# A third weight piece moved behind the evictions, and two value scalings moved between GpSimd and VectorE

## The chip, the core and the metric

The kernel runs on one core of a Trainium2 chip. The metric is device time in microseconds (us) of one execution, median over several runs. The engines are named as the profile names them: PE is TensorE's matrix unit and PEld its weight loads, DVE is VectorE, ACT is ScalarE, POOL is GpSimd, SP is SyncE, which issues most of the DMAs.

## What is computed

Two parts follow each other. The first is a linear attention ("retention") with a decay per head, over 4 batches, 8 heads, 768 positions and head width 64:

```python
for t in range(S):
    state = gamma[None, :, None, None] * state + np.einsum('bhd,bhe->bhde', k[:, :, t], v[:, :, t])
    y[:, :, t] = scale * np.einsum('bhd,bhde->bhe', q[:, :, t], state)
```

Its 3072 rows of 512 numbers go into a layer of 8 experts, where each row goes to one expert only:

```python
logits = x @ w_gate
expert_idx = np.argmax(logits, axis=1)
# probs = softmax(logits); gate_w = probs of the chosen expert
for e in range(E):
    xe = x[expert_idx == e]
    out[expert_idx == e] = gate_w[expert_idx == e, None] * (np.maximum(xe @ w1[e], 0.0) @ w2[e])
```

## The kernel before

**Chunks and periods.** The attention is cut into 24 chunks of 128 positions (6 for a batch). The loop over `n` (line 615) makes 12 periods, 0 to 11, of two chunks each, `a = 2n` and `b = 2n + 1`. The recurrence over positions is turned into matmuls: `scores` (line 278) multiplies keys and queries into the PSUM banks `sp`, and DVE masks them into `Sb` (line 287); `update` (line 293) adds a chunk to the state `U`, which ACT copies to `ub`; `carry` (line 313) multiplies the queries with the state into the PSUM tile `Y`, and `output` (line 330) adds the chunk's own part. `evict` (line 340) takes `Y` out of PSUM on DVE, into `xT`. The decay is carried by scaling: `scale` (line 265) multiplies a chunk's values by powers of gamma, and its result `vs` is read by `update` and `output`. There is one buffer for `Y`: the first matmul of `carry` for a period cannot start before both evictions of the period before have read it.

**Order.** The order is written by hand: every engine runs its instructions in the order in which the code names them, so an instruction that waits holds back all that follow it on its engine. POOL's queue holds most of the scalings, one for a chunk, and the scatter DMAs that send finished rows (line 853), with short dummy instructions between sends (`pause`, line 201, tile `idle`).

**What fills the gaps.** Beside the attention, the weights of the first expert are prepared: `split` (line 142) has ACT cast a piece of a loaded weight to `whi`, and an engine of the caller's choice subtracts it into `wlo` (line 148). `SPLITS` names the pieces of each period; period 7 has three, all subtracted on DVE: the first at line 640, the other two at line 648, ahead of `output` in the code and so ahead of the evictions on DVE.

**The early rows.** In period 9 (`soon`), after the send of chunk 17, SP fetches the rows already known to belong to the first expert (`fetch_early`, line 526, tile `xg`). In period 11 DVE transposes them (line 868), ACT casts them to `xh` (line 875), and PE begins that expert with them (line 908) before the attention has ended. The seven other experts follow from line 1131 on, and take most of the run.

**Which engine scales which chunk.** Chunk 0 is scaled in halves, heads 0 to 3 on POOL, heads 4 to 7 on DVE (line 290, between two maskings). All others are scaled on POOL by `scale`: chunk 1 near the start (line 606), chunks 21 and 22 together at the end of period 9 (lines 708 and 710).

Of the kernel before, what the change touches and what calls it, by code (L numbers as in the profile page):

```python
# [10 lines left out]
F32 = mybir.dt.float32  # L11
# [7 lines left out]
B, H, S, D = 4, 8, 768, 64  # L19
E, DM, F = 8, 512, 1024  # L20
N = B * S
P = 128
# [38 lines left out]
SPLITS = {n: tuple(next(_ORDER) for _ in range(c)) for n, c in _PIECES.items()}  # L61
# [48 lines left out]
def retention_moe(ctx, tc, front, qkv, w1, w2, first_rows, second_rows, out):  # L110
    nc = tc.nc
# [30 lines left out]
    def split(pos, part, i, engine, n=2):  # L142
        if i == 0:
            wparts[pos, part] = [wp.tile([P, 4, 512], F32R, name=n, tag="w", bufs=11) for n in ("whi", "wlo")]
        raw, (hi, lo) = raws[pos, part], wparts[pos, part]
        h = slice(n * i, n * i + n)
        nc.scalar.copy(out=hi[:, h], in_=raw[:, h])  # L147
        engine.tensor_tensor(out=lo[:, h], in0=raw[:, h], in1=hi[:, h].bitcast(F32), op=ALU.subtract)  # L148
# [74 lines left out]
    with ExitStack() as actx:  # L223
        apool = lambda name, bufs, **kw: actx.enter_context(tc.tile_pool(name=name, bufs=bufs, **kw))
        ld = apool("ld", AHEAD)
        wk = apool("wk", 2)
# [22 lines left out]
        def turned(g, i):  # L249
            return qs[g][:, i].rearrange("a (p t) -> a p t", p=NP)  # L250
# [6 lines left out]
        scaled = {}  # L257

        def scale_heads(g, engine, h):
            v, powers = (qs[g][:, 2], cv[:, g % CPB, :]) if g else (head[:, 0:DM], head[:, DM:DM + H])  # L260
            engine.tensor_tensor(
                out=scaled[g][:, h], in0=v.rearrange("a (h d) -> a h d", d=D)[:, h],
                in1=powers[:, h].unsqueeze(2).broadcast_to([P, h.stop - h.start, D]), op=ALU.mult)

        def scale(g):
            c = g % CPB
            vs = scaled[g] = wk.tile([P, H, D], F32, name="vs", bufs=3)
            scale_heads(g, nc.gpsimd, slice(0, H if g else H // 2))
            vss[g] = vs.rearrange("a (n t) d -> a n (t d)", t=2)
            if g == 1:  # L270
                double(2)
            if g == c and g > 0:
                grow(c)
# [4 lines left out]
        def scores(g):  # L278
            Sb = wk.tile([P, 2, NP, C], F32, name="Sb")
            q, kt = turned(g, 0), turned(g, 1)  # L280
            sps = [bank(2 * (g % 2) + r, "sp") for r in range(2)]
            for p in range(NP):
                for r in range(2):
                    nc.tensor.matmul(out=sps[r][:, p, :], lhsT=kt[half[r], p, :], rhs=q[half[r], p, :],  # L284
                                     start=True, stop=True)
            for r in range(2):
                nc.vector.tensor_tensor(out=Sb[:, r], in0=sps[r],  # L287
                                        in1=causal.unsqueeze(1).broadcast_to([P, NP, C]), op=ALU.mult)
                if g == 0 and r == 0:
                    scale_heads(0, nc.vector, slice(H // 2, H))  # L290
            Sbs[g] = Sb

        def update(g):
# [16 lines left out]
        def begin(n):  # L310
            Ys[n] = ps_1.tile([P, 2, DM], F32, name="Y", tag="Y")
# [28 lines left out]
        def evict(g):  # L340
            Y, c = Ys[g // 2], g % CPB
            if g % 2 == 0:
                xTs[g // 2] = wk.tile([P, NP, TW], F32, name="xT")
            xT = xTs[g // 2][:, :, (g % 2) * C:(g % 2 + 1) * C]
            nc.vector.tensor_tensor(out=xT.rearrange("a (r m) t -> a r m t", m=2), op=ALU.mult,
                                    in0=Y[:, :, 2 * (g % 2) * C:2 * (g % 2 + 1) * C].rearrange("a r (m t) -> a r m t", m=2),
                                    in1=G[:, c].rearrange("a (r m) t -> a r m t", m=2))
# [264 lines left out]
        soon = FULL // 2  # L612
        stages = {}

        for n in range(last + 1):
            a, b = 2 * n, 2 * n + 1
            s = gating(chosen[n]) if n in chosen else None
            if s:
                stages[chosen[n]] = s
            begin(n)  # L620
            if n == soon:
                logits(n - 1)
            else:
                if n == 0:
                    output(a)
                carry(n)
            if n > 0:
                if n == last:
                    turn_early()
                if n != soon:  # L630
                    logits(n - 1)
                if n == last:
                    for j, w, _ in first["pieces"]:
                        cut_high(nc, first["x"][0], first["xt"], j, w)
                if n in AMID:
                    send_behind(state["LT"][:, 0:1], AMID[n])
                rows(a - 2, "s0")
                rows(a - 1, "s1")
                finish_logits(n - 1)
            for i in SPLITS[n][:1 if n == 7 else None] if n in (6, 7) else ():  # L640
                split(0, *i, nc.gpsimd if n == 6 else nc.vector, 1)
            if s and n < last:
                s["choose"]()
            if n == soon:
                carry(n)
            if b % CPB < CPB - 1:
                update(b)
            for i in SPLITS[n][1:] if n == 7 else ():
                split(0, *i, nc.vector, 1)
            if s and n < last:  # L650
                s["soft"]()
            if n > 0:
                output(a)
            if n == soon:
                s["rank"]()
            output(b)
            if n == soon:
                for name in ("slots", "weights", "label", "counts"):
                    s[name]()
                nc.vector.tensor_copy(out=filled, in_=full)  # L660
                nc.vector.tensor_scalar(out=s0, in0=full, scalar1=base, scalar2=float(EARLY), op0=ALU.subtract,
                                        op1=ALU.min)
                nc.vector.tensor_tensor(out=start, in0=s0, in1=base, op=ALU.add)
                send_apart(range(FULL - 2, FULL))
                fill_late()
                fetch_early()
            elif s and n < last:
                s["rank"]()
                s["slots"]()
                if n == GROUPS[0][1] // 2:  # L670
                    s["totals"]()
            for g in (a, b):
                evict(g)
            if n == last:
                cut_early()
                s["choose"]()
            elif s:
                for name in ("weights", "label")[2 * (n == soon):] + ("advance",):
                    s[name]()
            if n == soon - 1:  # L680
                scale(b + 2)
                scale(a + 4)
            if n in BEHIND:
                send_behind(xTs[n][:, 0, C:C + 1], BEHIND[n],
                            pause if n == soon - 1 else lambda: [scale(g) for g in ((b + 2, a + 4) if n == soon - 2 else (b + 2,))])
            if n == 1:
                nc.vector.tensor_scalar(out=run, in0=k_("ebase"), scalar1=1.0 / P, scalar2=None, op0=ALU.mult)
            if n < last:
                if n > 0:
                    update(a + 2)  # L690
                if n in AFTER:
                    pause()
                    send_behind(ubs[(a + 2) % 3][:, 0, 0:1], AFTER[n])
                scores(a + 2)
                if n == 0:
                    update(a + 2)
                scores(b + 2)
            if n == GROUPS[0][1] // 2:
                s["pick"]()
                expert_at[0] = nc.sync.value_load(first_at[0:1, 0:1], min_val=0, max_val=E - 1)  # L700
                fetch(0, 0)
                fill_rows()
                fetch(0, 2)
            if n == 0:
                nc.scalar.copy(out=wgs[:, :, 0:E], in_=k_("gates").rearrange("p (k e) -> p k e", k=NP))
            if n < last:
                if n not in BEHIND:
                    scale(b + 2)
                if n < last - 1 and n not in (soon - 2, soon - 1):
                    scale(a + 4)  # L710
            for i in SPLITS.get(n, ()) if n > 7 else ():
                split(0, *i, nc.gpsimd, 1)
            for g in (a, b):
                if FIRST <= g < NCH - AHEAD - len(MID):
                    load(g + AHEAD + len(MID))
                if g in fetches:
                    fetch(0, fetches[g])
                for i in LATER.get(g, ()):
                    load(i)
# [650 lines left out]
```

## Time and profile before

| | us |
|---|---|
| median of 3 runs | 381.54 (381.48 to 381.74) |
| the profiled execution, its own time | 379.4 |
| its span, from the first instruction to the last | 377.6 |
| PE busy in the span | 371.0 (98%) |
| POOL busy | 260.3 (69%) |
| DVE busy | 251.7 (67%) |
| ACT busy | 140.5 (37%) |

The mean granted TensorE clock was 0.997. The page says where time is spent in total. The rows further down are from the list of instructions in order of time: a row gives start and duration in us, engine, line, operation, `out<-in` and shape, the count of instructions merged into the row, and in square brackets how long the engine was idle before it and what ended that. A row's end is its start plus its duration. The end of a matmul row is modelled; back to back, a row starts a little before the modelled end of the one before.

### The profile page before, as it was taken

How to read it: one execution, taken by the hardware profiler on the slowest of the kernel's cores; microseconds unless marked ns; L12 is line 12 of the kernel's file. 1: busy time of each engine (PE TensorE's matmuls, PEld its weight loads, DVE VectorE, ACT ScalarE, POOL GpSimd, SP SyncE). 2: the span in 40 equal slices, each digit the busy share in tenths (PEclk: the TensorE clock that was granted, in tenths of full speed). 3: DMA queues.
4: the chain of work that ended last, by engine and by line, in shares of the span. 5: the costliest groups of instructions: out<-in, count | busy, mean ns of one | idle time of the engine just before them, and what ended most of it. 6: DMA issues, size and time to landing. Idle time of an engine off the chain costs nothing. (4 is left out here: it accounts for less than half of the span.)

```text
span 377.6 us, 8710 instructions
## 1 busy us (share of the span) xinstructions
PE 371.0 (98%) x3279; PEld 349.3 (93%) x3279; DVE 251.7 (67%) x496; ACT 140.5 (37%) x252; POOL 260.3 (69%) x278
## 2 busy tenths in 40 slices
PE   8999999999999999999999999999999999999994
PEld 5888888788899899999999999999999999999984
DVE  3467858877778866768784777576676668667211
ACT  2222344244541645534630543154235316424200
POOL 3751669988760299008996999499569929987873
PEclk9999999999999999999999999999999999999998
DMA  7999999986249597869646754846457557520102
GB/s 305 417 414 420 416 402 423 417 353 172 92 159 201 197 240 252 262 217 277 223 145 115 231 162 141 194 166 210 133 149 224 176 91 251 184 101 24 38 20 80
DMA packets 42031, 82.06 MB, mean 217 GB/s; under 512 B 4268, under 2 KB 17584, under 8 KB 39537
## 3 DMA queue, kind: packets, MB, share of 16 engines
q1 hardware_dynamic: 36656, 67.67, 54.4%
q0 software_dynamic: 5312, 13.49, 10.0%
q8 instruction: 47, 0.77, 0.9%
q14 instruction: 16, 0.12, 0.1%
HBM read 65.80 MB, written 15.85 MB: 216 GB/s over the span
## 5 line engine op out<-in xcount | busy, mean ns | idle before, releaser
L853 POOL DMA_INDIRECT out<-Z,sidx x88 | 100.9, 1147 | 63.9 <-DVE Z L1061 49.2
L148 DVE TENSOR_TENSOR wlo<-raw,whi 128x1024 fp32r<-128x1024 f32 (+1 forms) x63 | 74.0, 1178 | 16.5 <-ACT whi L147 16.2
L203 POOL TENSOR_TENSOR idle<-cs 1x256 bf16<-1x256 f32 x102 | 79.6, 780 | 2.8
L147 ACT CAST whi<-raw 128x1024 fp32r<-128x1024 f32 (+1 forms) x72 | 67.7, 951 | 5.8 <-DMA raw<-w 5.8
L1218 PE MATMUL py<-hh,whi 128*128 128x392 f32 (+4 forms) x192 | 65.7, 342 | 0.0
L1218 PE MATMUL py<-hl,whi 128*128 128x392 f32 (+4 forms) x192 | 65.7, 342 | 0.0
L1218 PE MATMUL py<-hh,wlo 128*128 128x392 f32 (+4 forms) x192 | 65.7, 342 | 0.0
L1193 ACT ACTIVATE hh<-ph 128x452 fp32r<-128x452 f32 (+6 forms) x56 | 28.4, 507 | 77.6 <-PE ph L1186 77.1
L1186 PE MATMUL ph<-xh,wlo 128*128 128x392 f32 (+5 forms) x224 | 49.0, 340 | 0.0
L1186 PE MATMUL ph<-xl,whi 128*128 128x392 f32 (+5 forms) x224 | 48.9, 340 | 0.0
L1186 PE MATMUL ph<-xh,whi 128*128 128x392 f32 (+5 forms) x224 | 48.9, 340 | 0.0
L1194 DVE SCALAR_TENSOR_TENSOR hl<-ph,hh 128x452 fp32r<-128x452 f32 (+6 forms) x56 | 32.1, 574 | 20.3 <-ACT hh L1193 19.5
L1186 PEld LDWEIGHTS ph<-xh,whi 128*128 128x128 f32 x224 | 40.2, 188 | 0.4
L1186 PEld LDWEIGHTS ph<-xl,whi 128*128 128x128 f32 x224 | 40.3, 188 | 0.2
L1186 PEld LDWEIGHTS ph<-xh,wlo 128*128 128x128 f32 x224 | 40.2, 188 | 0.1
L1218 PEld LDWEIGHTS py<-hl,whi 128*128 128x128 f32 x192 | 36.1, 188 | 0.2
L1218 PEld LDWEIGHTS py<-hh,wlo 128*128 128x128 f32 x192 | 36.1, 188 | 0.2
L1218 PEld LDWEIGHTS py<-hh,whi 128*128 128x128 f32 x192 | 36.0, 188 | 0.2
L287 DVE TENSOR_TENSOR Sb<-sp,cs 128x512 f32<-128x512 f32 x48 | 29.9, 681 | 5.9 <-PE sp L284 5.9
L875 ACT CAST xh<-buf 128x512 fp32r<-128x512 f32 (+6 forms) x24 | 13.3, 558 | 51.5 <-DVE buf L868 51.5
L853 POOL DMA_INDIRECT x_sorted<-xrow,KEY x24 | 24.9, 1037 | 6.9 <-issue 4.1
L1056 DVE STREAM_TRANSPOSE Z<-py 128x416 f32<-128x416 f32 (+3 forms) x24 | 15.0, 625 | 18.9 <-PE py L1218 18.5
(200 smaller groups left out, 555.6 us busy)
## 6 DMA issues: line engine op xcount, KB each, us to landing
raw<-w SPq DMA_DIRECT2D x32, 1024.0 KB, 6.1
qkv_w<-qkv SPq DMA_DIRECT2D x12, 1024.0 KB, 17.7
qkv_t<-qkv SPq DMA_DIRECT2D x7, 1024.0 KB, 15.1
qkv_t<-front SPq DMA_DIRECT2D x7, 512.0 KB, 7.5
buf<-x_sorted SPq DMA_DIRECT2D x12, 211.2 KB, 5.2
x_sorted<-cs SPq DMA_DIRECT2D x7, 260.0 KB, 5.5
buf<-x_sorted SPq DMA_DIRECT2D x8, 195.0 KB, 3.9
out<-Z,sidx POOLq DMA_INDIRECT x88, 3.6
```

The lines of the kernel that those rows point to most:

```text
L147: nc.scalar.copy(out=hi[:, h], in_=raw[:, h])
L148: engine.tensor_tensor(out=lo[:, h], in0=raw[:, h], in1=hi[:, h].bitcast(F32), op=ALU.subtract)
L203: nc.gpsimd.tensor_tensor(out=idle[0:1], in0=cs[0:1, 0:PAUSE], in1=cs[0:1, 0:PAUSE], op=ALU.mult)
L287: nc.vector.tensor_tensor(out=Sb[:, r], in0=sps[r], in1=causal.unsqueeze(1).broadcast_to([P, NP, C]), op=ALU.mult)
L853: sc = tc.nc.gpsimd.indirect_dma_start(out=dst, out_offset=bass.IndirectOffsetOnAxis(ap=index, axis=0), in_=rows, in_offset=None, bounds_c ...
L875: nc.scalar.copy(out=xh[:, :, c0:c0 + w], in_=xt[:, :, t0:t0 + w])
L1056: nc.vector.transpose(out=Zs[e][:, 0:nb, k, :], in_=py[:, 0:32 * nb].rearrange("p (j c) -> p j c", c=32))
L1186: nc.tensor.matmul(out=ph[:, :w], lhsT=wparts[e, f // 4][a][:, kd, fo:fo + P], rhs=x[:, kd, :w], start=(n == 0), stop=(n == 3 * KD - 1))
L1193: nc.scalar.activation(out=hh[:, :cap], in_=ph[:, :cap], func=AF.Relu)
L1194: nc.vector.scalar_tensor_tensor(out=hl[:, :cap], in0=ph[:, :cap], scalar=0.0, in1=hh[:, :cap].bitcast(F32), op0=ALU.max, op1=ALU.subtract)
L1218: nc.tensor.matmul(out=py[:, :c], lhsT=a[:, f % 4, k * P:(k + 1) * P], rhs=x[:, :c], **se)
```

## The change

Three places change. The third weight piece of period 7 is no longer subtracted ahead of that period's evictions but behind them, and the two matching ACT casts keep their order. Chunk 21 is scaled on DVE, at the same place in the code, which on DVE is behind the four maskings of period 9. Chunk 1 is scaled in halves as chunk 0 was: heads 0 to 3 on POOL, heads 4 to 7 on DVE between the two maskings of chunk 1. Nothing is computed differently.

```diff
         def scale_heads(g, engine, h):
+            if g not in scaled:
+                scaled[g] = wk.tile([P, H, D], F32, name="vs", bufs=3)
...
-        def scale(g):
+        def scale(g, engine=nc.gpsimd):
             c = g % CPB
-            vs = scaled[g] = wk.tile([P, H, D], F32, name="vs", bufs=3)
-            scale_heads(g, nc.gpsimd, slice(0, H if g else H // 2))
+            scale_heads(g, engine, slice(0, H // 2 if g < 2 else H))
+            vs = scaled[g]
...
-                if g == 0 and r == 0:
-                    scale_heads(0, nc.vector, slice(H // 2, H))
+                if g < 2 and r == 0:
+                    scale_heads(g, nc.vector, slice(H // 2, H))
...
-            for i in SPLITS[n][1:] if n == 7 else ():
+            for i in SPLITS[n][1:2] if n == 7 else ():
                 split(0, *i, nc.vector, 1)
...
             for g in (a, b):
                 evict(g)
+            for i in SPLITS[n][2:] if n == 7 else ():
+                split(0, *i, nc.vector, 1)
...
-                    scale(b + 2)
+                    scale(b + 2, nc.vector if n == soon else nc.gpsimd)
```

DVE at the end of period 7, before: masking of chunks 14 and 15, the reduction of the logits, the three pieces, the two evictions, and the masking of chunks 16 and 17 (the names `Sb`, `wlo` and `xT` are those of the section on the kernel; `lg` holds logits).

```order
L287 TENSOR_TENSOR Sb<-sp,cs 128x512 x4
L408 TENSOR_REDUCE lg_1120<-lp 128x16
L148 TENSOR_TENSOR wlo<-raw,whi 128x512 x3
L345 TENSOR_TENSOR xT<-Y,buf 128x4x128 x2
L287 TENSOR_TENSOR Sb<-sp,cs 128x512 x4
```

DVE at the same place, after (all lines behind the edits are numbered two to four higher):

```order
L289 TENSOR_TENSOR Sb<-sp,cs 128x512 x4
L410 TENSOR_REDUCE lg_1121<-lp 128x16
L148 TENSOR_TENSOR wlo<-raw,whi 128x512 x2
L347 TENSOR_TENSOR xT<-Y,buf 128x4x128 x2
L148 TENSOR_TENSOR wlo<-raw,whi 128x512
L289 TENSOR_TENSOR Sb<-sp,cs 128x512 x4
```

One piece stands between the evictions and the maskings now, where it stood ahead of the evictions.

POOL from the last sends of period 9 to the weight pieces, before: the send of chunk 17 is the last DMA, the two scalings behind it are chunks 21 and 22.

```order
L853 DMA x_sorted<-xrow,KEY 25600x520 x2
L203 TENSOR_TENSOR idle<-cs 1x256
L853 DMA x_sorted<-xrow,KEY 25600x520
L261 TENSOR_TENSOR vs<-qkv_t,cs 128x512 x2
L148 TENSOR_TENSOR wlo<-raw,whi 128x512 x2
```

DVE at the end of period 9, after: evictions of chunks 18 and 19, a sum of counts, the masking of chunks 20 and 21, the scaling, and period 10's logits.

```order
L347 TENSOR_TENSOR xT<-Y,buf 128x4x128 x2
L470 TENSOR_REDUCE tot_1478<-EA 128x8
L289 TENSOR_TENSOR Sb<-sp,cs 128x512 x4
L263 TENSOR_TENSOR vs<-qkv_t,cs 128x512
L410 TENSOR_REDUCE lp<-lp 128x16
```

One `vs` has left POOL, where chunk 22's now follows the send at once, and stands on DVE behind the maskings.

## Rows read from the trace of the kernel before

**Rows 1.** Waits of PE: line, waited for whom, us, times, longest.

```profile
PE U L301 <- POOL vs L261: 0.3, 1, 0.3
PE Y L323 <- DVE xT L345: 0.3, 1, 0.3
```

**Rows 2.** In order of time, end of period 7 (columns as told above).

```profile
64.86 2.06 PE L284 MATMUL sp<-qkv_t 64*128 64x128 f32 x32
...
65.81 1.27 DVE L345 TENSOR_TENSOR xT<-Y,buf 128x512 f32<-128x512 f32 x2
66.22 0.60 POOL L203 TENSOR_TENSOR idle<-cs 1x256 bf16<-1x256 f32 x1
66.98 1.02 POOL L853 DMA_INDIRECT x_sorted<-xrow,KEY  x1 [0.16 <-issue]
67.01 2.47 DVE L287 TENSOR_TENSOR Sb<-sp,cs 128x512 f32<-128x512 f32 x4
67.23 1.10 PE L323 MATMUL Y<-qkv_t,ub 64*64 64x128 f32 x32 [0.32 <-DVE xT L345]
...
68.84 1.10 PE L356 MATMUL tr<-cs,xT 128*128 128x128 f32 x8
```

**Rows 3.** The same join of PE one period earlier, without a wait.

```profile
58.19 1.06 PE L284 MATMUL sp<-qkv_t 64*128 64x128 f32 x16
...
59.18 0.67 PE L323 MATMUL Y<-qkv_w,ub 64*64 64x128 f32 x16
```

**Rows 4.** In order of time, end of period 9 and start of period 10.

```profile
81.74 2.47 DVE L287 TENSOR_TENSOR Sb<-sp,cs 128x512 f32<-128x512 f32 x4
...
83.58 1.01 POOL L853 DMA_INDIRECT x_sorted<-xrow,KEY  x1 [0.16 <-issue]
...
84.62 2.05 POOL L261 TENSOR_TENSOR vs<-qkv_t,cs 128x512 f32<-128x512 f32 x2
...
85.02 0.38 PE L402 MATMUL lp<-cs,LT 128*128 128x128 f32 x2
...
85.73 0.69 PE L301 MATMUL U<-vs,qkv_t 128*64 128x64 f32 x16 [0.33 <-POOL vs L261]
```

**Rows 5.** The early rows' way to PE, in order of time.

```profile
87.10 2.96 SPq L157 DMA_DIRECT2D xg<-x_sorted  x4
...
92.96 1.30 DVE L868 STREAM_TRANSPOSE xt<-xg 128x512 f32<-128x512 f32 x2 [0.18 <-DMA xg<-x_sorted]
...
93.71 1.16 ACT L875 CAST xh<-xt 128x512 fp32r<-128x512 f32 x2 [0.58 <-DVE xt L868]
...
95.70 0.71 PE L908 MATMUL ph<-xh,whi 128*128 128x240 f32 x4
```

**Rows 6.** Scatter DMAs from 60 to 100 us: count, median us to landing.

```profile
x_sorted<-xrow,KEY POOLq DMA_INDIRECT x14, 7.1
```

**Rows 7.** DVE and POOL at the same time, in order of time, four places.

```profile
39.76 1.71 DVE L489 TENSOR_TENSOR behind<-cs,which 128x7 f32<-128x7 f32 x1
...
63.07 1.06 POOL L261 TENSOR_TENSOR vs<-qkv_t,cs 128x512 f32<-128x512 f32 x1
63.15 1.53 DVE L148 TENSOR_TENSOR wlo<-raw,whi 128x512 fp32r<-128x512 f32 x1 [0.79 <-ACT whi L147]
...
64.89 1.31 POOL L853 DMA_INDIRECT x_sorted<-xrow,KEY  x1 [0.16 <-issue]
...
124.03 1.01 POOL L853 DMA_INDIRECT x_sorted<-cs,pads  x1 [0.16 <-issue]
...
124.47 0.69 DVE L882 TENSOR_TENSOR xl<-buf,xh 128x512 fp32r<-128x512 f32 x1 [0.58 <-ACT xh L875]
```

**Rows 8.** In order of time, chunk 1.

```profile
7.32 0.42 DVE L261 TENSOR_TENSOR vs<-head 128x256 f32<-128x256 f32 x1
...
8.64 1.04 POOL L261 TENSOR_TENSOR vs<-qkv_t,cs 128x512 f32<-128x512 f32 x1 [0.28 <-DMA qkv_t<-front]
...
9.80 0.69 PE L301 MATMUL U<-vs,qkv_t 128*64 128x64 f32 x16
```

## The prediction

> **What bounds the kernel now.** I read the page first: PE is busy for 98% of the span (the table ahead), so only time in which PE stands still can be won, and a shorter stretch on DVE or POOL is worth nothing by itself. The second view is the list of PE's waits [rows 1]. Beside the start of the run it has two entries: PE waits once for DVE's evictions (line 323) and once for a scaling on POOL (line 301), 0.3 us each. The change goes at exactly these two. So the sum is short, and the question is what PE meets next. For that I read the order of time around each wait [rows 2, 4] and the path of the early rows behind them [rows 5].
>
> **The third weight piece.** In period 7 DVE subtracts three pieces, then evicts twice (65.81 to 67.08). PE ends the scores at 64.86 + 2.06 = 66.92 and starts the carry at 67.23, because the one `Y` buffer is free only then [rows 2]. One period earlier the same join has no wait: the scores end at 58.19 + 1.06 = 59.25 by the model, and the carry starts at 59.18, 0.07 before that [rows 3]. So the wait costs 67.23 - 66.92 + 0.07 = **0.38 us**. With the piece behind them, the evictions end about 0.6 earlier (two of them take 1.27, so one instruction is some 0.6 from start to start), near 66.5, ahead of PE's 66.85. The whole 0.38 goes.
>
> The piece itself costs PE nothing, but it lands badly. It reaches DVE near 66.4, while POOL runs a dummy (66.22 to 66.82). Where a DVE instruction on two SBUF tensors met a running POOL instruction, it stood until that ended: the first piece started at 63.15 beside a scaling that ran to 64.13, took 1.53, and ended 0.55 after it [rows 7]. So the moved piece should end near 67.4, and the maskings behind it start near 67.3 instead of 67.01. What hides this is PE's own work: the transposes (68.84 before, 68.46 now) need the first two maskings, done by 67.3 + 1.3 = 68.6, and the second half of the transposes starts near 68.9. Without that cover up to 0.3 would come back. POOL pays too. Its send at 66.98 would meet the running piece; the send at 64.89 met one and took 1.31 instead of 1.01 [rows 2, 7]. So POOL's queue runs some 0.3 late from there, and as it is full up to the send of chunk 17, that send moves from 83.58 to about 83.9 [rows 4].
>
> **Chunk 21 on DVE.** PE ends the logits' transposes at 85.02 + 0.38 = 85.40 and starts the update of chunk 21 at 85.73, released by POOL's scaling [rows 4]. With the same 0.07 this is **0.40 us**. Gone from POOL is 2.05 / 2 = 1.03. On DVE the scaling stands behind the maskings, which end at 84.21, now 0.38 earlier: 83.83. A DVE instruction of this shape with two SBUF operands takes 0.69 (the one at 124.47) [rows 7], so it ends near 84.5. PE asks for it at 85.73 - 0.40 - 0.38 = 84.95, so 0.4 is spare and the wait goes. What is queued behind it on DVE, the reduction of the logits, waits for PE's transposes until 85.0 anyway.
>
> Here too POOL is met. DVE's scaling starts at 83.8, and the send of chunk 17 near 83.9. If DVE is first, the send stands until 84.5 and is another 0.45 late (0.6 of overlap, less the 0.1 by which the send at 64.89 got on before its piece ended). If the send is first, neither suffers: a send at 124.03 took its usual 1.01 with a DVE instruction started inside it, and that one took 0.69 [rows 7]. So the send ends 0.3 to 0.75 later than before.
>
> The Trainium skill bears on this: "SBUF — State Buffer", section "SBUF: two separate sides", says that a DVE instruction with two SBUF inputs and a GpSimd instruction take a shared pair of ports as an exclusive lock, whichever starts first, and that descriptors of a DMA issued from GpSimd cannot be written while DVE holds it. The rows with 1.53 and 1.31 agree, the one of 1.01 at 124.03 shows no such loss. By the skill's rule alone the send would lose time in either order, and the second rival below would be the forecast.
>
> **What is late next.** The fetch of the early rows stands behind the send of chunk 17 in the code and reads what it writes. SP issues it at 87.10, 2.5 after the send's end; the rows arrive for DVE at 92.96 (which had waited only 0.18), and ACT ends their cast at 93.71 + 1.16 = 94.87. PE starts on them at 95.70 [rows 5], so 0.83 is spare. After two gains PE comes at 95.70 - 0.78 = 94.92: the spare time is used up, and any delay of the send that reaches the fetch now costs PE one to one. The bounds of that are 0 (all of it lost in the DMA queues) and 0.7 (0.75 less the 0.05 left). In this stretch a send lands 7.1 after its issue (median of 14), of which its own instruction is 1.0 [rows 6], so most of the way is queueing and I take a value near the lower end: **0.2 us** given back. Everything after it follows PE.
>
> **Chunk 1.** POOL's scaling ran from 8.64 to 9.68 and PE's update started at 9.80 [rows 8]. Halved, POOL is done near 9.2; DVE's half (0.42 for chunk 0's) may stand until then and end near 9.5; the masking that it holds back ends near 10.15, and PE wants that after the update, at 9.80 + 0.69 = 10.49. All is hidden, and the time won on POOL is won ahead of loads that it must wait for. I count 0; bounds are 0.1 either way. If the load came 0.3 later than in this execution, the masking would be late; before, POOL's full scaling would have been late as well.
>
> **Sum.** The profiled execution took 379.4 (span 377.6): 379.4 - 0.38 - 0.40 + 0.2 = 378.8, a gain of 0.58. On the median of the three runs, 381.54, the same gain gives 380.95 (0.15%). A measurement of this kernel tells some 0.2% from no change, which is 0.76 us; the gain is likely below that.
>
> **Rivals.**
> - Both waits go and nothing comes back: 0.78, with a little from chunk 1 up to 0.84, so 380.75. For it: the queueing in [rows 6] and that the send may start first. Chance 0.25.
> - The early rows take all of it back: the delay of the send, 0.75, reaches the fetch in full, PE waits at line 908, and the time is about 381.5. For it: DVE had waited for just these rows [rows 5], and the lock rows. Against it: DVE's scaling must start in the 0.1 before the send. Chance 0.17.
> - The first wait stays, because another release lies behind the evictions: only 0.40 is won, and the early rows' spare time is not touched: 381.15. Against it: the evictions are what the row names [rows 2]. Chance 0.07.
> - **Slower:** DVE's scaling of chunk 21 is shut out by POOL. There is one row for it: a DVE instruction of 7 columns started at 39.76 inside a send, took 1.71 and ended with the scaling that POOL had taken up behind that send [rows 7]. Here it would stand until chunk 22's scaling ends (83.9 + 1.0 + 1.05 = 85.95), and end 0.55 later, 86.5. PE's update would start at 86.6 instead of 85.73, 0.87 later than before, the first gain eaten with it: 382.4. It decides from the point at which DVE has not got in before chunk 22's scaling starts (84.9, a good 1.0 behind the forecast start). Chance 0.06.
>
> **How the numbers follow.** The forecast, a gain of 0.4 to 0.7, has 0.45. The predicted time is its 380.95. The range goes from 380.65 (0.84 won, and 0.05 for the spread of the runs) to 381.55 (nothing won); outside it lie the slower case and some 0.06 at both edges. Faster by over 0.2% is about half of the first rival and a little of the forecast, 0.2; slower by over 0.2% is the last rival and a remainder, 0.07; the rest, 0.73, is within 0.2%.
>
> **What would show it.** In the profile after: PE's list of waits without the two entries; the carry of period 8 starting 0.07 before the end of the scores; the third piece on DVE taking over 0.9, beside a POOL dummy, and the send behind it 1.3; chunk 21's scaling on DVE done before 84.6 and PE's update of it with no wait. For the given-back part: a wait of PE at line 908 for ACT's cast, some 0.2, and SP's fetch later than 87.10. The prediction is wrong if PE waits nowhere there (more is won), or waits 0.7 (nothing is), or if DVE's scaling lasts over 1.5.

## The result, and the profile after

The changed kernel takes **383.64 us** in the median (383.51 to 385.33, six runs) against 381.52 for the kernel before beside it: 2.1 us slower in the median, where 380.95 was predicted. The ratio is 1.0067, with an interval of 1.0047 to 1.0086; this and all ratios below are of the means of the runs.

Read the list of PE's waits in the profile after first (columns as in [rows 1]).

```profile
PE U L303 <- DVE vs L263: 2.0, 1, 2.0
...
PE U L303 <- POOL vs L263: 0.7, 1, 0.7
PE Y L325 <- issue: 0.6, 2, 0.3
```

Both entries of [rows 1] are gone: no row waits for the evictions, and the row with POOL's scaling is another one, at chunk 0. At the top stands a wait that was not there: 2.0 us for a scaling on DVE. That is chunk 21's, the one that the change moved.

The end of period 7, in order of time (start, us, engine, line, operation), answers to [rows 2]:

```profile
64.94 2.06 PE L286 MATMUL sp<-qkv_t 64*128 64x128 f32 x32
...
65.18 1.27 DVE L347 TENSOR_TENSOR xT<-Y,buf 128x512 f32<-128x512 f32 x2
...
66.38 0.97 DVE L148 TENSOR_TENSOR wlo<-raw,whi 128x512 fp32r<-128x512 f32 x1
...
66.92 1.10 PE L325 MATMUL Y<-qkv_t,ub 64*64 64x128 f32 x32
66.96 1.28 POOL L857 DMA_INDIRECT x_sorted<-xrow,KEY  x1 [0.16 <-issue]
```

This half went as the sum had it. The evictions start 0.63 earlier, the carry starts 0.08 before the modelled end of the scores (64.94 + 2.06 = 67.00) where it had started 0.31 behind it, the moved piece takes 0.97, and the send beside it 1.28 instead of 1.02.

The end of period 9 and the start of period 10 answer to [rows 4]:

```profile
83.08 0.72 PE L325 MATMUL Y<-qkv_t,ub 64*64 64x128 f32 x11
...
83.80 1.01 POOL L857 DMA_INDIRECT x_sorted<-xrow,KEY  x1 [0.16 <-issue]
...
84.11 0.44 PE L325 MATMUL Y<-qkv_t,ub 64*64 64x128 f32 x4 [0.31 <-issue]
...
84.15 1.29 DVE L289 TENSOR_TENSOR Sb<-sp,cs 128x512 f32<-128x512 f32 x2 [1.02 <-PE sp L286]
84.84 1.06 POOL L263 TENSOR_TENSOR vs<-qkv_t,cs 128x512 f32<-128x512 f32 x1
84.86 0.27 PE L325 MATMUL Y<-qkv_t,ub 64*64 64x128 f32 x1 [0.31 <-issue]
...
85.35 3.54 DVE L263 TENSOR_TENSOR vs<-qkv_t,cs 128x512 f32<-128x512 f32 x1
...
85.84 2.49 POOL L148 TENSOR_TENSOR wlo<-raw,whi 128x512 fp32r<-128x512 f32 x2
...
88.94 0.69 PE L303 MATMUL U<-vs,qkv_t 128*64 128x64 f32 x16 [2.00 <-DVE vs L263]
```

DVE's scaling was expected to take 0.69. It takes 3.54, and ends at 88.89, 0.56 behind the end of POOL's two weight pieces (85.84 + 2.49 = 88.33). PE starts the update of chunk 21 at 88.94 instead of 85.73, 3.2 later. The traces stand 381.9 - 377.6 = 4.3 apart; the rest is 0.5 at a stop of PE at 113 us and 0.5 at the end of the run, both taken up below, and less than 0.2 of drift.

DVE comes late to the scaling in this trace. Its second pair of maskings waits 1.02 for PE's scores and starts at 84.15, so by the record the scaling starts at 85.35, 0.51 behind POOL's scaling of chunk 22. In the other traces with the loss, below, it starts ahead of POOL's, and loses all the same.

PE also loses time here without an engine to blame: the 16 matmuls of this carry, 0.67 us at another period [rows 3], come in three pieces over 2 us, with two stops that the list calls "issue". They are taken up last; they hide in the wait, which would else be nearer 3.4.

### The profile page after: what moved, and what is told of

Its sections match the earlier page's. It is cut to its first block, busy times and chain, and to the rows that moved or that the text cites. A ratio compares the mean times of both kernels' runs of the same rounds, so it can differ in the third digit from the quotient of the medians.

```text
span 381.9 us, 8712 instructions
## 1 busy us (share of the span) xinstructions
PE 371.8 (97%) x3279; PEld 348.7 (91%) x3279; DVE 256.6 (67%) x498; ACT 140.5 (37%) x252; POOL 259.1 (68%) x277
```

## Experiments: which part costs the time

Theory 1: POOL shuts DVE's scaling of chunk 21 out. Theory 2: the moved weight piece makes the loss, since it delays POOL. Theory 3: the halves of chunk 1 do. The level of the kernel before differs between the sets of runs that were made together (379.6 in three of them, 381.1 in one, 381.5 beside the result above), so every number below is compared within its set.

The kernel before again, first against itself:

> The kernel before, unchanged. Its profiled execution took 379.4, the median of its other runs 381.5, and after's profiled one 383.75 against a median of 383.64. If the 2.1 between the first two belong to a lower mean granted clock in the runs that were not profiled (two of the six runs of after had 0.992 where the others had 0.999, and were 1.6 longer), the clocks listed for this kernel's runs show it: 379.4 at 0.997 or more, 381 and over below 0.995. If not, the clock is the same in short and long runs.

It took 379.54 beside 379.57 (ratio 0.9998, 0.9989 to 1.0007). None of its runs is near 381.5, so what made that median is not answered by it. The first part of the change alone:

```diff
-            for i in SPLITS[n][1:] if n == 7 else ():
+            for i in SPLITS[n][1:2] if n == 7 else ():
...
             for g in (a, b):
                 evict(g)
+            for i in SPLITS[n][2:] if n == 7 else ():
+                split(0, *i, nc.vector, 1)
```

> Only the third piece is moved; chunk 21 and chunk 1 are scaled on POOL as before. Theory 1 (the loss is the scaling of chunk 21 on DVE, shut out by POOL): 0.3 to 0.4 us less than before, PE starts the carry of period 8 without a wait, and waits for POOL's scaling of chunk 21 by 0.3 to 0.6. Theory 2 (the loss is from the moved piece, which makes POOL's queue 0.2 late and brings the stall of 1.4 us that PE shows in the carry of period 10): 1 to 2 us more than before, with the stall in the trace.

Measured 379.79, 0.22 more than before (1.0007, 0.9998 to 1.0015), which can't be told from no change. Its trace in order of time, with the same place in the kernel before of that set under it:

```profile
67.21 1.10 PE L325 MATMUL Y<-qkv_t,ub 64*64 64x128 f32 x32
...
71.10 0.85 PEld L338 LDWEIGHTS Y<-Sb,vs 128*64 128x64 f32 x16 [0.19 <-POOL vs L263]
...
84.21 1.01 POOL L857 DMA_INDIRECT x_sorted<-xrow,KEY  x1 [0.16 <-issue]
...
86.36 0.69 PE L303 MATMUL U<-vs,qkv_t 128*64 128x64 f32 x16 [0.81 <-POOL vs L263]
```

```profile
67.39 1.10 PE L323 MATMUL Y<-qkv_t,ub 64*64 64x128 f32 x32 [0.31 <-DVE xT L345]
...
83.74 1.01 POOL L853 DMA_INDIRECT x_sorted<-xrow,KEY  x1 [0.16 <-issue]
```

The first wait goes: PE had come 0.20 later into this period and still starts the carry 0.18 earlier. But POOL is late from there on. PE's weight loads wait for its scaling already in period 8's output (0.19, at 71.10; the matmuls come 0.12 later by it), which the prediction had not looked at; the send of chunk 17 starts at 84.21 instead of 83.74, and the wait for POOL's scaling of chunk 21 grows from 0.33 to 0.81. What was won at one engine's wait comes back at another's.

The second part alone, chunk 21's scaling given to DVE:

```diff
-                    scale(b + 2)
+                    scale(b + 2, nc.vector if n == soon else nc.gpsimd)
```

> Only chunk 21 goes to DVE. Without the moved piece the maskings end at 84.2 if PE does not stall, and POOL takes up chunk 22's scaling at 84.6. Theory 1 in its plain form (DVE is shut out here whatever stands ahead): 2 us or more above before, DVE's scaling takes 3 us or more. Theory 2 (it is shut out only because the maskings came 1.0 late by PE's stall in the carry, which the moved piece brings): DVE gets in at 84.2, takes 0.7, and the time is 0.3 to 0.4 below before.

Measured 383.98 (1.0108, 1.0089 to 1.0127), 4.4 more than before. This part makes the loss by itself:

```profile
84.27 4.53 DVE L263 TENSOR_TENSOR vs<-qkv_t,cs 128x512 f32<-128x512 f32 x1
84.76 1.06 POOL L263 TENSOR_TENSOR vs<-qkv_t,cs 128x512 f32<-128x512 f32 x1
...
85.76 2.48 POOL L148 TENSOR_TENSOR wlo<-raw,whi 128x512 fp32r<-128x512 f32 x2
...
88.86 1.12 PE L303 MATMUL U<-vs,qkv_t 128*64 128x64 f32 x16 [3.31 <-DVE vs L263]
```

DVE starts 0.49 ahead of POOL's scaling of chunk 22 by the record, and yet stands over all three POOL instructions, to 88.80. The other way round, the whole change without this part:

```diff
-                    scale(b + 2, nc.vector if n == soon else nc.gpsimd)
+                    scale(b + 2)
```

> The piece moved and chunk 1 in halves, chunk 21 on POOL as before. Theory 1: all of the loss is gone, 0.3 to 0.4 below before. Theory 2: 1 to 2 us above before remain. Theory 3 (the halves of chunk 1 upset the start, where after shows a wait of PE for POOL of 0.7 that before has not): above the kernel with the moved piece alone by 0.2 or more.

Measured 380.25, 0.68 more than before (1.0016, 1.0006 to 1.0026). Theory 2 falls as the cause of the large loss; a smaller one is left, of which the piece's 0.22 may be a part. For the rest, chunk 1's halves alone, with the kernel before again beside them (the argument `engine` of `scale` is as in the change):

```diff
-            scale_heads(g, nc.gpsimd, slice(0, H if g else H // 2))
+            scale_heads(g, engine, slice(0, H // 2 if g < 2 else H))
...
-                if g == 0 and r == 0:
-                    scale_heads(0, nc.vector, slice(H // 2, H))
+                if g < 2 and r == 0:
+                    scale_heads(g, nc.vector, slice(H // 2, H))
```

> The kernel before again. The chips differ: one ran it in 379.57, one in 381.13, the one of the prediction's median in 381.5. If this chip is of the slower kind, its trace should hold short stops of PE with no releaser between 75 and 85 and near 110, some 1.5 in all, which the trace of before (379.4) has not, and which after's trace showed in the carry of period 10 (1.4); the stop in after's trace is then the chip's and not the change's. If the chip is of the quick kind (379.6), the trace has none, and the question stays open.

> Chunk 1 in halves alone. Theory 3 (the halves win 0.1 to 0.2 at the start, and the end of the run is 0.48 longer, since in the three kernels with them the span ends 5.28 behind PE's last matmul and in the six without them 4.80): 0.3 more than before, the trace ending 5.28 behind PE. Rival (the longer end came with other edits): 0.1 to 0.2 less than before, the trace ending 4.80 behind PE.

Before took 379.64 beside 379.71 (0.9996, 0.9987 to 1.0005); the halves 380.02, 0.31 more (1.0007, 0.9998 to 1.0016). By the interval alone this can't be told from no change; the traces tell it. Two rows, the last send in the trace of the kernel before of this set and in that of the halves:

```profile
373.76 1.01 POOL L853 DMA_INDIRECT out<-yo,pair  x1 [1.80 <-DVE yo L1040]
```

```profile
373.61 1.01 POOL L855 DMA_INDIRECT out<-yo,pair  x1 [1.80 <-DVE yo L1042]
```

The last send is 0.15 earlier with the halves; PE's update of chunk 1 had come 0.1 earlier. The span ends 0.33 later all the same, at 378.07 instead of 377.74. From PE's last matmul to the end it is 5.28 in all six traces with the halves and 4.80 in all those without them, and the difference lies behind the start of the last send: 4.46 from there to the end instead of 3.98. Why the end of the program takes 0.48 longer was not tried; it is open.

## Experiments: what shuts DVE out

Theory 1 has branches: a dummy shuts DVE out like a scaling (1a) or doesn't (1b); the send itself shuts DVE out (1c) or only a ready instruction behind it (1d). All kernels of this section have chunk 21's scaling alone on DVE, and the edits are to that kernel. In the first, POOL's two weight pieces come behind PE's update of chunk 21, so that one POOL instruction is left behind the send:

```diff
+            for i in SPLITS[9] if n == 10 else ():
+                split(0, *i, nc.gpsimd, 1)
...
-            for i in SPLITS.get(n, ()) if n > 7 else ():
+            for i in SPLITS.get(n, ()) if n > 9 else ():
```

> Chunk 21 alone on DVE, as in e1_c21, but POOL's two weight pieces of period 9 (and their casts) come behind chunk 21's update, so that on POOL only chunk 22's scaling follows the send of chunk 17. Theory 1 (DVE stands until the row of POOL instructions ends, whatever its length): DVE's scaling starts at 84.3, ends 0.56 behind chunk 22's, near 86.4, 2.1 long instead of 4.5; PE's update at 86.45 instead of 88.86, 0.55 later than before, so some 380.1. Rival (it waits for something else, the early rows or DVE's own queue): it stays at 4 or more, and the time at 382.5 or more.

Measured 381.24, 0.1 more than before (1.0007, 0.9998 to 1.0016).

```profile
84.98 1.91 DVE L263 TENSOR_TENSOR vs<-qkv_t,cs 128x512 f32<-128x512 f32 x1
85.27 1.06 POOL L263 TENSOR_TENSOR vs<-qkv_t,cs 128x512 f32<-128x512 f32 x1
```

DVE now stands over one instruction only, and again ends 0.56 behind it (86.89, 86.33). PE doesn't wait for it, but PE comes to it some 1.3 late in this set, by the stops that are taken up last; so the time doesn't price the one instruction. Now the other direction, a dummy on POOL ahead of chunk 22's scaling, a fourth instruction of 1 x 256 numbers:

```diff
                     scale(b + 2, nc.vector if n == soon else nc.gpsimd)
+                if n == soon:
+                    pause()
```

> Chunk 21 alone on DVE, and one more dummy on POOL (1 partition, 0.60) between the send of chunk 17 and chunk 22's scaling. Theory 1a (the send itself does not shut DVE out; what did in e1_c21 was that the next POOL instruction was ready and took the port): if the dummy takes it as well, DVE's scaling lasts until the pieces end, 0.75 longer than in e1_c21, 5.2, and the time is near 383.3 or above. Theory 1b (a dummy does not, as at 124.47 of the kernel before, where a DVE instruction inside a send with a dummy behind it took its usual 0.69): DVE's scaling takes 0.7, PE does not wait at chunk 21's update, and the time is 379.2.

Measured 385.52, 4.4 more (1.0115, 1.0097 to 1.0133).

```profile
84.36 1.01 POOL L857 DMA_INDIRECT x_sorted<-xrow,KEY  x1 [0.16 <-issue]
84.73 5.26 DVE L263 TENSOR_TENSOR vs<-qkv_t,cs 128x512 f32<-128x512 f32 x1
...
85.39 0.60 POOL L203 TENSOR_TENSOR idle<-cs 1x256 bf16<-1x256 f32 x1
85.97 1.03 POOL L263 TENSOR_TENSOR vs<-qkv_t,cs 128x512 f32<-128x512 f32 x1
86.97 2.48 POOL L148 TENSOR_TENSOR wlo<-raw,whi 128x512 fp32r<-128x512 f32 x2
```

The dummy shuts this DVE instruction out like the others: DVE does not get in between send and scaling, and stands over all four. In each of these cases DVE starts inside a send. Whether the send itself does it, or only what stands ready behind it, is told apart by holding everything behind the send back until PE's update of chunk 21, by a copy that reads the update's output:

```diff
+            if n == 10:
+                nc.gpsimd.tensor_copy(out=gated, in_=ubs[b % 3][:, 0, 0:1])
+                scale(a + 2)
+                for i in SPLITS[9]:
+                    split(0, *i, nc.gpsimd, 1)
...
-                if n < last - 1 and n not in (soon - 2, soon - 1):
+                if n < last - 1 and n not in (soon - 2, soon - 1, soon):
...
-            for i in SPLITS.get(n, ()) if n > 7 else ():
+            for i in SPLITS.get(n, ()) if n > 9 else ():
```

> Chunk 21 alone on DVE behind the maskings, as in e1_c21, with chunk 22's scaling and the two pieces both held behind chunk 21's update, so that POOL stands still after the send of chunk 17. Theory 1c (the send itself shuts DVE out): DVE's scaling starts in the send and ends 0.56 behind the send's end, about 1.0 long. Theory 1d (only a tensor instruction that stands ready behind the send does): it takes 0.69. Both have PE waiting little or not at all for chunk 21, and a time of 379.2 to 379.6 on a chip where before takes 379.57 (0.3 less to no change).

Measured 379.30, **0.41 less** than before (0.9986, 0.9977 to 0.9995).

```profile
83.98 1.02 POOL L860 DMA_INDIRECT x_sorted<-xrow,KEY  x1 [0.16 <-issue]
...
84.49 0.68 DVE L263 TENSOR_TENSOR vs<-qkv_t,cs 128x512 f32<-128x512 f32 x1
...
85.69 0.69 PE L303 MATMUL U<-vs,qkv_t 128*64 128x64 f32 x16
```

DVE starts in the middle of the send again, and takes 0.68; the send takes its usual 1.02; PE does not wait for the scaling. So the send is no obstacle. For this instruction the one behind it is, if it is ready: with 0, 1, 3 and 4 ready instructions of POOL the same DVE instruction took 0.68, 1.91, 4.53 and 5.26.

It is no rule for every DVE instruction. In the trace of the kernel before, 42 instructions of lines 148 and 882, with two SBUF inputs each, start inside a send that has a ready dummy behind it, as here:

```profile
198.96 1.01 POOL L853 DMA_INDIRECT out<-Z,sidx  x1 [0.16 <-DVE buf L868]
...
199.63 0.69 DVE L882 TENSOR_TENSOR xl<-buf,xh 128x512 fp32r<-128x512 f32 x1 [0.69 <-ACT xh L875]
...
199.99 0.80 POOL L203 TENSOR_TENSOR idle<-cs 1x256 bf16<-1x256 f32 x1
```

All 42 take their usual time (0.69 for 512 columns, 1.18 to 1.23 for 1024). It is the dummy that stands: it ends 0.47 to 0.50 behind DVE, and takes up to 1.5 instead of 0.60. The row at 124.47 that the prediction followed is one of them. DVE can also get in between two POOL instructions: its half of chunk 1, in the kernel with the halves alone,

```profile
8.72 0.61 POOL L263 TENSOR_TENSOR vs<-qkv_t,cs 128x256 f32<-128x256 f32 x1 [0.35 <-DMA qkv_t<-front]
...
8.85 0.76 DVE L263 TENSOR_TENSOR vs<-qkv_t,cs 128x256 f32<-128x256 f32 x1
...
9.29 0.80 POOL L598 TENSOR_TENSOR buf<-buf,cs 128x256 f32<-128x256 f32 x1
```

stands over the first of them only and ends at 9.61; the next one is longer instead (0.80; 0.61 in the kernel before of that set). So a ready instruction behind the send was needed for the loss here, but is not enough by itself. What tells chunk 21's scaling, and the instruction at 39.76 [rows 7], from those that got in was not tried.

The Trainium skill, "SBUF — State Buffer", section "SBUF: two separate sides", has a DVE instruction with two SBUF inputs and a GpSimd instruction that reads SBUF share a pair of ports under an exclusive lock, which whoever starts first keeps for the whole instruction. The traces agree that one stands while the other works, and at the 42 places the first to start won. They do not agree on the length at chunk 21: DVE stood over a whole row of POOL instructions (4.53 for three). By their recorded starts, the one that started first also lost there, by 0.3 to 0.7 us, in five traces.

The same page's section has GpSimd's descriptors of a DMA shut out while a DVE instruction in a two-port mode holds the lock. Whether a scaling runs in such a mode no run shows. Where it was first, a send did lose: in the kernel with the scaling ahead of the maskings, below, the send that started 0.26 into DVE's scaling took 1.27 instead of 0.98. In the order send first, DVE second, nothing was lost (1.02 and 0.68).

The Trainium skill, "Perfetto Trace Analysis", section "GPSIMD Engine Instruction", draws the reported start of such an instruction at its read, behind the begin of its execution. That would let POOL be first in truth and second in the record; no run here shows the time between the two, and why POOL wins stays open.

## Experiments: how 3 us become 5, and how to get them back

The whole change was run again in two other sets:

> The changed kernel again, on the chip on which the kernel before takes 379.57 (the median of before that the prediction had was 381.5). If the gap between the two medians, 2.1, understated the change because the two traces stand 4.3 apart, it takes 383.5 here (4 us more than before). If a part of the trace's gap was of that one execution (the stall of 1.4 us in PE's carry of period 10 with no releaser), it takes 382 to 382.5 and the new trace has no such stall.

> The changed kernel once more, for a comparison on one chip with the two below. DVE's scaling of chunk 21 should stand until the pieces end, PE's update of it start 3 to 3.5 later than before, and the time be 3.5 above before where the granted clock stays up, 5 or more where it falls after PE's stand. If the chip is of the quick kind (before near 379.6) and the stop of PE in the carry of period 10 is the chip's, the trace has none there; if the change makes it, it is there again.

It took 386.33 (5.2 more than before; 1.0138, 1.0124 to 1.0153) and 384.66 (5.0 more; 1.014, 1.0125 to 1.0156), where it had been 2.1 more in the result above. In the second of these two sets there is a trace of the kernel before as well:

> The kernel before, for its trace on this chip. On a chip of the slower kind (above 381) it has short stops of PE with no releaser between 72 and 86 and near 110, some 1.5 in all, as the four traces of the second set of runs have. On a quick one it has none, and whether before has them on the slower chips stays untested.

In order of time, the whole change of that set, and under it the kernel before:

```profile
84.37 4.70 DVE L263 TENSOR_TENSOR vs<-qkv_t,cs 128x512 f32<-128x512 f32 x1
...
89.12 1.12 PE L303 MATMUL U<-vs,qkv_t 128*64 128x64 f32 x16 [3.79 <-DVE vs L263]
...
90.03 3.05 PE L338 MATMUL Y<-Sb,vs 128*64 128x128 f32 x32
...
93.27 0.69 PE L303 MATMUL U<-vs,qkv_t 128*64 128x64 f32 x16
```

```profile
85.83 0.69 PE L301 MATMUL U<-vs,qkv_t 128*64 128x64 f32 x16 [0.37 <-POOL vs L261]
86.35 1.92 PE L336 MATMUL Y<-Sb,vs 128*64 128x128 f32 x32
...
88.46 0.69 PE L301 MATMUL U<-vs,qkv_t 128*64 128x64 f32 x16
```

The update of chunk 21 is 3.29 late (89.12 - 85.83), that of chunk 22 already 4.81 (93.27 - 88.46). Between them nobody waits; the matmuls themselves are slower, 1.12 instead of 0.69 and 3.05 instead of 1.92. The windows of two us, with the granted clock as the column behind POOL's, show why:

```profile
88.00:90.00 2.00, 0.88 (x16) 0.88 (x18) 1.86 (x6) 0.00 (x0) 0.51 (x1) 0.73 0.61 144
90.00:92.00 2.00, 2.00 (x26) 2.00 (x24) 0.31 (x3) 0.49 (x2) 0.00 (x0) 0.50 0.87 170
92.00:94.00 2.00, 2.00 (x41) 1.74 (x39) 0.59 (x3) 0.00 (x0) 1.04 (x1) 0.91 1.01 342
```

At the end of the 3.8 us in which PE stood the granted clock is 0.50, 1.2 of 2.4 GHz, and returns only near 92. That is another 1.5 us. With the 0.48 at the end of the run it makes the whole of the distance between the traces: 3.29 + 1.52 + 0.48 = 5.3 (382.9 - 377.6).

How much of it is the clock varies from run to run. With chunk 21 on DVE alone, two runs with a mean clock of 1.000 took 382.5 and 382.7, 3.0 more than before, which is the wait (3.31 - 0.33); the run of its profile, with a mean clock of 0.988, took 384.9. Not every run fits: one of that kernel took 383.9 at 0.998, and one of the whole change 384.5 at 0.999, 1.4 and 1.1 more than the wait and the longer end make, and what they met is open. In the profiles the clock fell after waits of 2.93, 3.31 and 3.79 (once each); it stayed up after one of 2.83, and after the one of 2.00 in the result above. Four other runs of the kernel with 2.83 show 0.988 to 0.995. It fell 1.4 and 0.2 before the end of the waits of 3.31 and 3.79, and 1.2 after PE had gone on behind the one of 2.93.

The hold that freed DVE was then put into the whole change:

> All three parts of the change, with one thing undone that stands behind the send of chunk 17 on POOL: chunk 22's scaling and the two pieces of period 9 are held until chunk 21's update is done. If the shutting out is all of the loss, DVE's scaling takes 0.68, PE does not wait for it, and of the change remain: 0.4 won there, 0.2 won by the piece (0.38 less 0.17 in period 8), 0.1 won at the start and 0.48 lost at the end by chunk 1: 0.2 less than before. If the piece or chunk 1 had a share in the loss, 1 or more above before.

Measured 379.38, 0.26 less than before (0.999, 0.9981 to 0.9999), and so 5.3 less than the change without it. PE's list of waits keeps, of all it had, the one at the start of the run that every kernel has:

```profile
PE warm L578 <- DVE ones L170: 1.1, 1, 1.1
```

Without chunk 1's halves as well:

> The same without chunk 1's halves. Theory: 0.4 won at chunk 21 and 0.2 by the piece, 0.6 less than before (0.9984), and no longer end. Rival (the later POOL queue, 0.47 by the piece, now holds up the sends and chunk 22's scaling): no better than e3_hold_all, 0.9986 to 1.000.

Measured 379.00, 0.64 less than before (0.9991, 0.9981 to 1.0001: the interval reaches no change). The two medians differ by 0.38, which fits the 0.31 that the halves cost alone.

There is a second way to give DVE the scaling without a fight: ahead of the maskings, and so ahead of the send of chunk 16 (again `scale` takes the engine, as in the change).

```diff
+                if n == soon:
+                    scale(b + 2, nc.vector)
                 scores(a + 2)
...
-                if n not in BEHIND:
+                if n not in BEHIND and n != soon:
```

> Chunk 21 alone on DVE, but its scaling stands ahead of the four maskings of period 9 instead of behind them. It starts at 81.9, just before the send of chunk 16 (82.0). Theory 1 (who is first has the port): 0.7 long, done by 82.6; the send of chunk 16 is lengthened to some 1.5; the maskings come 0.7 later, the last ends at 85.1, ahead of PE's output of chunk 20; PE waits nowhere in period 10 and the time is 0.3 below before, 379.25. Rival (DVE is too late by the 0.1 it needs to start, and stands through the send, the dummy and the next send): 2 or more long, the maskings late by that, 381 or more.

Measured 380.44, 0.69 less than before in its set (0.9982, 0.9973 to 0.9991), twice what was expected; where the rest comes from was not followed.

```profile
82.16 0.68 DVE L263 TENSOR_TENSOR vs<-qkv_t,cs 128x512 f32<-128x512 f32 x1
...
82.42 1.27 POOL L857 DMA_INDIRECT x_sorted<-xrow,KEY  x1 [0.31 <-ACT whi L147]
```

DVE is first and loses nothing; the send takes 0.29 longer. With the moved piece added:

> Chunk 21's scaling on DVE ahead of the maskings, and the third piece behind the evictions; chunk 1 as before. Theory (POOL's lateness by the piece, 0.47, cost PE only through POOL's scaling of chunk 21, which is now on DVE): the piece's gain of 0.38 less the 0.17 that period 8 lost comes on top of the 0.6 to 0.7 of e2_first: 0.8 to 0.9 less than before (0.9977). Rival (the late sends now hold up the early rows, or chunk 22's scaling on POOL is late): as e2_first or worse, 0.998 to 0.999.

Measured 379.38, 0.33 less than before, with three of twelve runs at 380.5 to 383.2 (1.0004, 0.9986 to 1.0022): it can't be told from no change. What those three runs met was not tried.

## The stops without a cause, and the size of the result

In the trace of the result's run PE stops in period 10's carry (some 1.4 us, in the rows above) and at 113 us (0.3 to 0.5, which the list puts to DVE). The traces of all four kernels of the set in which the kernel before took 381.1 have stops too, though at other matmuls: from the transposes at 75.7 to the logits near 86 they make PE 0.9 to 1.7 later than in the same or the nearest kernel of another set, and one of 0.3 stands between 110 and 115. Of those four only the whole change has the piece and the halves. Such stops stand in no trace of the three sets where the kernel before took 379.6, among them one on the same chip with the same kernel. So they belong to the set, not to the change and not to the chip as some expectations above have it, and a kernel before of 381.1 to 381.5 has most likely paid them too; a trace of it in such a set is lacking, so this is argued, not shown.

It would explain why the result above is +2.1 and the two other sets +5.0 and +5.2. Beside the result, the kernel before would pay the stops, while in the changed one they fall into PE's wait, which is 2.0 instead of 3.8, and the clock stays up in its profile (0.998). In the set at 381.1 the wait was 2.93 in spite of the stops, and the clock fell.

## Why the prediction was wrong, point by point

- **The first wait: right.** 0.38 was to go, and the carry starts 0.08 before the scores' end. The piece's 0.97 (over 0.9 expected) and the send's 1.28 (1.3 expected) were right too.
- **The piece's follow-up: its place was missed.** POOL's queue was to run 0.3 late, with all of it met at the early rows. With the piece alone it ran 0.47 late (0.31 in the whole change beside the trace of its set) and was met sooner, at the weights of period 8's output (0.19 at 71.10) and at the scaling of chunk 21. By itself the piece shows no gain, 0.22 lost within the spread, where 0.38 was to be won.
- **Chunk 21: the step that failed** is "If the send is first, neither suffers". It was taken from one row, where a DVE instruction inside a send took 0.69 [rows 7]. It is right for the send, as the kernel with everything held shows (0.68 in 1.02). But it left out what stands behind the send: here chunk 22's scaling and two weight pieces, ready. Beside them DVE's scaling took 3.54 to 4.70 where 0.69 was put, and the 0.40 became 3.3 of delay. A ready dummy stood behind the send of that row too, and did no harm, as at 41 other places: DVE instructions of that kind got in, and the scaling did not. Why is open.
- **The order at the send: put too early.** The maskings were to end 0.38 earlier, at 83.83, and DVE to come about as the send starts. In the whole change beside the trace of its set they end at 84.44 (81.97 + 2.47), 0.2 later than before, and DVE comes 0.38 into the send. One cause shows: a DVE instruction of one column ahead of the evictions takes 0.47 there instead of 0.16, beside a dummy of the late POOL queue, and the evictions start 0.18 later. So the branch that failed was the one that was taken.
- **The slower rival had the mechanism and under a fifth of its price.** It let DVE stand until chunk 22's scaling ends and decided at the point where that scaling starts (84.9). In the result's own trace DVE was late by that measure (85.35 behind 84.84). In three others it was on time (84.27, 84.37, 84.49) and should have been safe, but was not. Here a ready instruction behind the send was enough, and the price is the whole row: 3.29 instead of 0.87, then the clock, which no rival had (1.5).
- **The row that said so was in hand.** The instruction of 7 columns that took 1.71 [rows 7] started inside a send with a scaling behind it: the present case. It was given .06, and the row of 0.69, of the moved instruction's own shape, was followed. The shape was no guide; what is one is not known, as 42 instructions got in past a ready dummy.
- **The early rows: not there.** 0.2 was to come back. With the piece alone the send is 0.47 late, SP's fetch moved by 0.1 only, and no wait stands at line 912. PE comes later there too, but with the hold in the whole change it comes 0.4 earlier than before, and the list has no such wait either. Where the rest of the delay went was not followed.
- **Chunk 1: counted 0, measured 0.31 lost.** PE's update came 0.1 earlier, the bound that was given, though DVE's half took 0.76 and made POOL's next instruction longer. The loss is at the other end of the program, where it was not looked for.
- **The sum:** -0.38 - 0.40 + 0.2 = -0.58 was predicted (380.96 by these terms); in the set where both traces exist it is +5.3, of which 3.29 is PE's delay at chunk 21 by the shut-out, 1.52 the clock and 0.48 the end. Without the shut-out it is -0.26, and -0.64 without the halves too, with an interval that just reaches no change. So the gain that was read from the two waits was most likely there to be had; the change as written had it blocked by the ready row on POOL.

## What to carry to other kernels

Before an instruction with two SBUF inputs goes from POOL to DVE, read what POOL has ready at the moment at which DVE comes to it, behind a running DMA send as well: DVE may stand for that whole row, not for one instruction. Whether it does must be measured, since other instructions of the same shape got in. Put it ahead of the row, or hold the row back by something that it must wait for. And price a PE wait of some 3 us with what the clock may take on top, from a row where PE ran at 1.2 GHz.

## What was not expected of the hardware

- One DVE instruction of 0.68 us took 1.91, 3.54, 4.53 to 4.70 and 5.26 beside one, three, three and four POOL instructions and ended 0.54 to 0.57 behind the last. A dummy of 1 x 256 numbers at the head of the row did not let it in either.
- In five of these traces POOL won although its recorded start came 0.3 to 0.7 us after DVE's. Where nothing stood ready behind the send, DVE worked inside the send without loss to either. And 42 other DVE instructions of the kernel before started inside a send and got in ahead of the ready dummy behind it. What decides between the two is open.
- The granted clock fell to 0.50 around waits of PE of 2.93 to 3.79 us and stayed there for 3.4 us in two traces and 6.8 in one, with PE at work for most of it.
- The program's end took 0.48 longer in each trace with chunk 1's halves, which stand at its start. This is open.
- PE stopped for 0.9 to 1.7 us in all, mostly without a releaser, in every trace of one set, and not in three others.
